# Inverse transform over n1 by even and odd rows, with stacked high and low parts, in a Fourier and maxout kernel

## The chip, the cores and the metric

The kernel runs on one core of one Trainium2 chip. The metric is the device time of one execution in microseconds. Six names come up: TensorE (PE, with its weight loads as PEld), VectorE (DVE), ScalarE (ACT), GpSimd (POOL), and SyncE (SP), which issues most of the transfers.

## What is computed

For each of 8 batches of 3072 rows and 256 columns: a real Fourier transform along the rows, a complex product with a 256 x 256 matrix plus bias, a soft threshold, the inverse transform, and then a layer that takes the maximum of three products and multiplies it by a fourth matrix.

```python
X = np.fft.rfft(x, axis=1)
Yr = Xr @ w_r - Xi @ w_i + b_r
Yi = Xr @ w_i + Xi @ w_r + b_i
Yr = np.sign(Yr) * np.maximum(np.abs(Yr) - lam, 0.0)      # Yi likewise
y = np.fft.irfft(Yr + 1j * Yi, n=3072, axis=1)            # (8, 3072, 256)
t = y.reshape(24576, 256)
h = np.maximum(np.maximum(t @ w1, t @ w2), t @ w3)        # 768 columns
out = h @ w_out                                           # (24576, 256)
```

## The kernel before

The transform length is split as 3072 = 96 x 32 (n1 and n2). Stage a transforms over n1 (a 96-row product), stage b over n2 for each of the 96 rows in pairs, stage w multiplies by the complex matrix, stage q goes back over n2 and writes z to DRAM, and `inverse` goes back over n1 with the tables `ga_sb`. The layer of three products (`up`) and the last product (`down`) follow on the result y.

The main loop runs over 8 batches, 8 chunks of a batch (`NCH`; a chunk is 4 of the 32 n2, 384 rows of y) and 6 blocks of 128 of the 768 columns (`NF`). One step of it, called a slot, has three groups of `up` (i = 0, 1, 2) and a `down`. The stages a to q of later batches are fitted between these groups by a list of events: `at(pos, fn, i)` books a call at a position counted in slots, and `run_until(pos)` issues what is due. Batch 0 goes through the stages in a prologue ahead of the loop.

Nearly all products are made of a high and a low 16-bit part of each operand in three matmuls (`mm3`: high x high, high x low, low x high). A split is one ScalarE instruction for the high part and one VectorE instruction for the low part; the latter is put off by `later` and issued at the next `flush`, which stands after each group. `in_turn` keeps such a pair behind the last eviction of `up`. PSUM has the tags `up` (3 buffers), `dn` (2) and `ff` (3, for all stages by `ff_tile`).

The steps around the change:
- `load_z(b, c)` brings a chunk of z, 96 rows by 4 x 256, in one transfer on SP's queue; it is called at f = 1 of the chunk before.
- `split_z` makes zh and zl, at f = 3, in two pieces where a batch begins.
- `inverse` runs at f = 4, one half of d before the second group and the other behind the third. For each n2 it does `mm3` with z as the stationary operand (96 x 128) and 96 columns of `ga_sb` as the moving one. ScalarE and VectorE then write yh and yl straight from PSUM.
- Stage a has three forms: native 32-bit for the first two batches (q < `NATIVE`), split 32-bit parts for batches 2 and 3, and 16-bit parts from `HALF_X` on. The last needs the batch's scale ahead of time, so x is loaded twice, and `largest_m` takes the maximum in an earlier batch.
- SP issues its transfers in order. Besides z it has the loads of x (`xq`, `xm`) and a, and the moves of `ab` and `vb` between partitions in groups of four.

Of the kernel before, what the change touches and what calls it, by code (L numbers as in the profile page):

```python
# [20 lines left out]
SB, SG = 10, 20  # L21
# [4 lines left out]
def dft_tables():  # L26
# [53 lines left out]
    def halves(v, scale):  # L80
        v = v * 2.0**scale
        hi = v.astype(np.float16)
        return np.ascontiguousarray(np.stack([hi, (v - hi).astype(np.float16)], 1))

    return (
        fa.astype(np.float32),
        halves(ga, SG),
        halves(np.stack([np.concatenate([v, v]) for v in blocks], 1), SB),
# [6 lines left out]
def fourier_maxout_kernel(  # L95
# [14 lines left out]
    NATIVE = 2 * NCH  # L110
    HALF_X = 4 * NCH
    EARLY = NCH + 5
# [107 lines left out]
    def first_homes():  # L220
        g = ga_sb.bitcast(F32).rearrange("p i n m -> p (i n m)")
# [263 lines left out]
    def largest_m(q):  # L485
        b, q4 = divmod(q, NCH)
        with in_turn():
            nc.vector.tensor_reduce(
                out=batch(b, "x")[0:N1, q4:q4 + 1], in_=st.pop(("m", q)), axis=AX.X,
                op=ALU.max, apply_absolute_value=True,  # L490
            )
        if q4 == NCH - 1:
            scale_x(b, NCH)
            st[b, "xx"] = xx = small("xx", bufs=3)
            nc.vector.tensor_scalar(
                out=xx, in0=st[b, "sx"][0], scalar1=X_SCALE, scalar2=None, op0=ALU.mult
            )

# [329 lines left out]
    for q in range(EARLY, NB * NCH):  # L828
        b, i = divmod(q, NCH)
        p = i if b == 1 else 9 + 5.2 * i if b == 2 else (b - 2) * SLOTS + 5.6 * i + 2  # L830
        at(p - (3 if b == 1 else 5 if b == 2 else 8), load_x, q)
        at(p, split_x, q)
        at(p + 1, stage_a, q)
        if q >= HALF_X:
            p = (b - 3) * SLOTS + 5.6 * i + 5
            at(p - 4, load_m, q)
            at(p, largest_m, q)
    for b in range(1, NB):
        for k in range(-2, NJP + 1):
            p = 8 + 2.2 * (k + 2) if b == 1 else (b - 1) * SLOTS + 2.8 * (k + 2)  # L840
            for d, fn, i in (
# [22 lines left out]
    def split_z(b, pieces=1):  # L864
        zh = fft.tile([96, NQ, D], F16, name="zh", bufs=1)
        zl = fft.tile([96, NQ, D], F16, name="zl", bufs=1)
        w = NQ * D // pieces
        for i in range(pieces):
            with in_turn():
                split_later(  # L870
                    *(t.rearrange("p n d -> p (n d)")[:, i * w:i * w + w] for t in (zh, zl)),
                    st["zq"][:, i * w:i * w + w], st[b, "su"][0][0:96],
                )
        st["z"] = zh, zl

    def inverse(b, c, y=None, part=(0, KD)):
        zh, zl = st["z"]
        yh, yl = y or [ffn.tile([P, KD, NT], F16, name=n, bufs=2) for n in ("yh", "yl")]
        for h in range(*part):
            py = ff_tile("pi")  # L880
            for n2 in range(NQ):
                mm3(
                    py[:, n2 * N1:(n2 + 1) * N1], *(t[:, n2, h * P:(h + 1) * P] for t in (zh, zl)),
                    *(ga_sb[:, i, c * NQ + n2, :] for i in range(2)),
                )
                st["pi"] = st["mm"]
            split_later(
                *(t[:, h].rearrange("p (m n) -> p m n", n=NQ) for t in (yh, yl)),
                py[:, 0:NT].rearrange("p (n m) -> p m n", n=NQ), Y_SCALE,
            )  # L890
        return yh, yl
# [166 lines left out]
    for b in range(NB):  # L1058
        for c in range(NCH):
            nxt = (b, c + 1) if c + 1 < NCH else (b + 1, 0) if b + 1 < NB else None  # L1060
            for f in range(NF):
                pos = b * SLOTS + c * NF + f
                up(y, f, 0)
                flush()
                if nxt and f == 3:
                    split_z(nxt[0], 1 if nxt[1] else 2)
                if nxt and f == 4:
                    y_next = inverse(*nxt, None, (0, 1))
                run_until(pos - 2 / 3)
# [19 lines left out]
                run_until(pos)  # L1089
                if nxt and f == 1:  # L1090
                    load_z(*nxt)
# [37 lines left out]
```

## Time and profile before

| | us |
|---|---|
| median of 3 runs | 2025.78 (2024.03 to 2027.57) |
| the profiled execution | 2023.95 |
| its span in the profile | 2022.2 |
| TensorE busy | 2005.8 |
| VectorE busy | 1428.8 |
| ScalarE busy | 1046.5 |
| inverse, high part of y on ScalarE, 128 times | 61.9 |
| inverse, low part of y on VectorE, 128 times | 70.5 |

The profile is one execution on the chip. A group's line has the source line, the engine, the operation, output and inputs with their shapes, the count, the busy time in us and the mean ns of one, and after a second bar the idle time of the engine in front of it with what ended it. Matmuls are pipelined, so their durations overlap; how long TensorE takes for a run of them is read from the starts in the timeline. A line of windows gives a stretch, its length, the busy time of each engine with its count, the granted clock of TensorE, the share of the transfer engines, and GB/s.

### The profile page before, as it was taken

The page shows a single profiled execution, that of the slowest core. Times are in us where ns is not written, and L with a number is a line of the kernel's source. Part 1 is how long each engine was busy: PE and PEld are TensorE (multiplying, and loading weights), DVE is VectorE, ACT ScalarE, POOL GpSimd, SP SyncE. Part 2 cuts the span into 40 slices and gives each one's busy share as a digit, 9 for nine tenths or more (in the row PEclk, how much of TensorE's full clock was granted, in tenths as well). Part 3 has the DMA queues.
Part 4 walks back from the last instruction along what each step waited for, and adds up shares of the span by engine and source line. Part 5 has one row for each costly group of instructions (what it writes and reads, how often), then busy time and mean ns, then how long its engine had stood idle before and what let it go on. Part 6 is the DMA issues. An engine that isn't in the chain of part 4 may idle for free.

```text
span 2022.2 us, 40241 instructions
## 1 busy us (share of the span) xinstructions
PE 2005.8 (99%) x15822; PEld 1406.3 (70%) x15822; DVE 1428.8 (71%) x2733; ACT 1046.5 (52%) x2052; POOL 20.5 (1%) x75
## 2 busy tenths in 40 slices
PE   9999999999999999999999999999999999999999
PEld 5757777777766777676776777767777677776666
DVE  3887886688866877677875788757776577754454
ACT  5755654455545555455544565545554454543333
POOL 0000000000000000000000000000000000000000
PEclk9999999999999999999999999999999999999999
DMA  9744443355433454345442454333442333311110
GB/s 302 206 134 134 126 121 93 112 137 137 110 113 96 120 142 110 93 108 135 127 113 87 122 138 117 103 107 82 128 113 61 89 94 93 82 53 32 32 32 24
DMA packets 203664, 220.34 MB, mean 109 GB/s; under 512 B 20659, under 2 KB 178995, under 8 KB 203379
## 3 DMA queue, kind: packets, MB, share of 16 engines
q1 hardware_dynamic: 142707, 142.24, 26.9%
q10 hardware_dynamic: 59744, 72.11, 11.2%
q0 software_dynamic: 1024, 3.41, 0.5%
q8 instruction: 125, 2.05, 0.4%
q14 instruction: 64, 0.52, 0.1%
HBM read 99.98 MB, written 75.50 MB: 87 GB/s over the span
## 4 chain that ended last, share of the span: by engine, by line
PE 96%; DVE 2%; DMA 1%; ACT 1%; issue 0%; SPq 0%; ACTq 0%; DVEq 0%
PE pu L174 18%; PE pu L172 18%; PE pu L173 18%; PE pd L174 6%; PE pd L173 6%; PE pd L172 6%; PE py L172 3%; PE py L174 3%; PE py L173 3%; PE px L674 2%; PE pa L531 1%; PE pi L174 1%; PE pi L172 1%; PE pi L173 1%; PE pa L172 1%; PE pa L173 1%
## 5 line engine op out<-in xcount | busy, mean ns | idle before, releaser
L172 PE MATMUL pu<-yh,wuh 128*128 128x384 f16 x2304 | 751.8, 326 | 2.5 <-DVE c L905 1.0
L174 PE MATMUL pu<-yh,wul 128*128 128x384 f16 x2304 | 751.5, 326 | 0.0
L173 PE MATMUL pu<-yl,wuh 128*128 128x384 f16 x2304 | 751.3, 326 | 0.1
L166 ACT ACTIVATE hh<-h 128x384 f16<-128x384 f32 x384 | 200.4, 522 | 495.3 <-DVE h L908 494.1
L905 DVE TENSOR_TENSOR c<-pu,c 128x384 f32<-128x384 f32 x384 | 212.6, 554 | 251.5 <-PE pu L174 150.4
L174 PEld LDWEIGHTS <-wul 128*128 128x128 f16 x2304 | 225.4, 98 | 150.0 <-issue 1.0
L172 PE MATMUL pd<-woh,hh 128*128 128x256 f16 x1152 | 313.8, 273 | 0.0
L173 PE MATMUL pd<-wol,hh 128*128 128x256 f16 x1152 | 313.8, 273 | 0.0
L174 PE MATMUL pd<-woh,hh 128*128 128x256 f16 x1152 | 313.5, 273 | 0.0
L173 PEld LDWEIGHTS <-wuh 128*128 128x128 f16 x2304 | 225.7, 98 | 125.4 <-issue 4.1
L172 PEld LDWEIGHTS <-wuh 128*128 128x128 f16 x2304 | 225.6, 98 | 125.3 <-issue 4.6
L167 DVE SCALAR_TENSOR_TENSOR hh<-h,hh 128x384 f16<-128x384 f32 x384 | 213.6, 556 | 138.9 <-ACT hh L166 136.6
L902 ACT ACTIVATE c<-pu 128x384 f32<-128x384 f32 x384 | 187.2, 488 | 187.6 <-PE pu L174 165.8
L908 DVE TENSOR_TENSOR h<-pu,c 128x384 f32<-128x384 f32 x384 | 211.8, 551 | 46.5 <-PE pu L174 42.6
L172 PE MATMUL py<-wch,tt 128*128 128x256 f16 x504 | 137.4, 273 | 0.0
L174 PE MATMUL py<-wch,tt 128*128 128x256 f16 x504 | 137.3, 272 | 0.0
L173 PE MATMUL py<-wcl,tt 128*128 128x256 f16 x504 | 137.3, 272 | 0.0
L172 PEld LDWEIGHTS <-hh 128*128 128x128 f16 x1152 | 112.7, 98 | 33.8 <-issue 0.3
L173 PEld LDWEIGHTS <-hh 128*128 128x128 f16 x1152 | 112.7, 98 | 33.4
L174 PEld LDWEIGHTS <-hh 128*128 128x128 f16 x1152 | 112.7, 98 | 13.7 <-DVE hh L167 0.5
L937 ACT ACTIVATE o<-pd,s1u 128x256 f32<-128x256 f32 x191 | 82.7, 467 | 75.1 <-PE pd L174 35.5
L167 DVE SCALAR_TENSOR_TENSOR zl<-zq,s0u,zh 96x1024 f16<-96x1024 f32 (+1 forms) x72 | 83.0, 1157 | 4.3 <-ACT zh L166 4.2
(219 smaller groups left out, 2635.6 us busy)
## 6 DMA issues: line engine op xcount, KB each, us to landing
z_d<-zs ACTq DMA_DIRECT2D x96, 256.0 KB, 2.9
out_dram<-o ACTq DMA_DIRECT2D x190, 128.0 KB, 2.1
zq<-z_d SPq DMA_DIRECT2D x63, 384.0 KB, 3.9
ab<-a_d SPq DMA_DIRECT2D x84, 256.0 KB, 4.1
ab<-ab SPq DMA_DIRECT2D x336, 64.0 KB, 2.1
xq<-in_x_dram SPq DMA_DIRECT2D x55, 384.0 KB, 3.9
a_d<-aq ACTq DMA_DIRECT2D x53, 384.0 KB, 3.3
vb<-vb SPq DMA_DIRECT2D x308, 64.0 KB, 2.4
```

The costliest lines, as they stand in the source:

```text
L166: nc.scalar.activation(out=hi, in_=src, func=AF.Copy, scale=scale)
L167: later(lambda: low(nc.vector.scalar_tensor_tensor(out=lo, in0=src, scalar=scale, in1=h, op0=ALU.mult, op1=ALU.subtract)))
L172: nc.tensor.matmul(o, lh, rh, start=start, stop=False, **kw)
L173: nc.tensor.matmul(o, lh, rl, start=False, stop=False, **kw)
L174: st["mm"] = nc.tensor.matmul(o, ll, rh, start=False, stop=stop, **kw)
L531: nc.tensor.matmul(pa[0:96], fr, xp, start=True, stop=True)
L674: nc.tensor.matmul(pv[:, h, :, g // 2, g % 2], ah[:, g // 2, g % 2, h * P:(h + 1) * P], mb_sb[:, i, 4 * kb + g].rearrange("p (c m) -> p c ...
L902: st["act"] = nc.scalar.activation(out=c1, in_=p, func=AF.Copy)
L905: st["dve"] = nc.vector.tensor_tensor(out=c1, in0=p, in1=c1, op=ALU.max)
L908: st["dve"] = nc.vector.tensor_tensor(out=h32, in0=p, in1=st["c1"], op=ALU.max)
L937: nc.scalar.activation(out=o, in_=pd[t], func=AF.Copy, scale=st[b, "su"][1])
```

## The change

The inverse table has a symmetry over n1: moving n1 by 48 multiplies the term of frequency k1 by +1 or -1 as k1 is even or odd. The changed `inverse` uses it. The 96 rows of z are sorted into 48 of even and 48 of odd frequency; each kind is multiplied by 48 columns of the table only, and the two results are added for the first 48 values of n1 and subtracted for the others.

High and low part of 48 rows fill 96 partitions together. So one matmul with `ga`'s high part takes both high x high and low x high, and a second one with its low part takes the rest (low x low comes along). For a half of d this is 2 kinds x 4 n2 x 2 = 16 matmuls of 48 columns where 4 x 3 = 12 of 96 columns stood. To stack the parts, `load_z` places the rows by kind in two transfers, `split_z` splits as before, and four transfers in SBUF bring the halves of zh and zl together. Behind the matmuls ScalarE copies the even result, VectorE forms sum and difference, ScalarE makes yh of them and VectorE yl.

In the loop `load_z` moves from f = 1 to f = 0, `split_z` from f = 3 to f = 2, the first half of the inverse from f = 4 to the end of f = 3, and the second from the end of f = 4 to behind its second group. The events are set a little closer (2.72 slots for 2.8 a step, 2.13 for 2.2 in batch 1). Batch 3's stage a changes to 16-bit parts (`HALF_X`), and the scale of such a batch is computed one slot behind the last maximum (`scale_m`).

```diff
+    m = np.arange(96)
+    ga = np.stack([ga[m % 4 >= 2, :, 0:48], ga[m % 4 < 2, :, 0:48]], 1)
...
-        halves(ga, SG),
+        np.concatenate([halves(ga, SG)] * 2),
...
-    HALF_X = 4 * NCH
+    HALF_X = 3 * NCH
...
-    ga_sb = const.tile([96, 2, N2, N1], F16, name="ga_sb")
+    ga_sb = const.tile([96, 2, 2, N2, N1 // 2], F16, name="ga_sb")
...
-        if q4 == NCH - 1:
-            scale_x(b, NCH)
...
+    def scale_m(b):
+        scale_x(b, NCH)
...
         if q >= HALF_X:
-            p = (b - 3) * SLOTS + 5.6 * i + 5
+            p = 9 + 5 * i if b == 3 else (b - 3) * SLOTS + 5.5 * i + 5
             at(p - 4, load_m, q)
             at(p, largest_m, q)
+            if i == NCH - 1:
+                at(p + 1, scale_m, b)
...
-            p = 8 + 2.2 * (k + 2) if b == 1 else (b - 1) * SLOTS + 2.8 * (k + 2)
+            p = 8 + 2.13 * (k + 2) if b == 1 else (b - 1) * SLOTS + 2.72 * (k + 2)
...
     def load_z(b, c):
...
-        for r in (slice(0, 88), slice(88, 96)) if b == c == 0 else (slice(0, 96),):
-            st["lz"] = ld = nc.sync.dma_start(out=zv[r], in_=batch(b, "z")[r, c * NQ:(c + 1) * NQ, :])
+        rows = batch(b, "z").rearrange("(j m) n d -> j m n d", m=4)
+        for j in (slice(0, 22), slice(22, 24)) if b == c == 0 else (slice(0, 24),):
+            for e in range(2):
+                st["lz"] = ld = nc.sync.dma_start(
+                    out=zv[48 * e + 2 * j.start:48 * e + 2 * j.stop],
+                    in_=rows[j, 2 - 2 * e:4 - 2 * e, c * NQ:(c + 1) * NQ, :],
+                )
...
     def split_z(b, pieces=1):
...
+        both = [
+            fft.tile([P, 2, D], F32, name="ze", tag=tag, bufs=3)[0:96].rearrange("p a d -> p (a d)").bitcast(F16)
+            for tag in ("vl", "vh")
+        ]
...
+            def move(cols=cols):
+                for i, t in enumerate((zh, zl)):
+                    for e in range(2):
+                        nc.sync.dma_start(
+                            out=both[e][48 * i:48 * i + 48, cols], in_=t[48 * e:48 * e + 48, cols]
+                        )
+
+            later(move)
...
     def inverse(b, c, y=None, part=(0, KD)):
...
-            for n2 in range(NQ):
-                mm3(
-                    py[:, n2 * N1:(n2 + 1) * N1], *(t[:, n2, h * P:(h + 1) * P] for t in (zh, zl)),
-                    *(ga_sb[:, i, c * NQ + n2, :] for i in range(2)),
+            for e in range(2):
+                for n2 in range(NQ):
+                    for i in range(2):
+                        st["pi"] = st["mm"] = nc.tensor.matmul(
+                            pv[:, e, n2], st["z"][e][:, n2, h * P:(h + 1) * P],
+                            ga_sb[:, i, e, c * NQ + n2], start=i == 0, stop=i == 1,
+                        )
...
+            nc.scalar.activation(
+                out=even, in_=py[:, 0:NT // 2], func=AF.Copy, scale=Y_SCALE
+            )
+
+            def halves(h=h, even=even, y32=y32, pv=pv):
...
+                for e in range(2):
+                    nc.vector.scalar_tensor_tensor(
+                        out=yv[:, e], in0=pv[:, 1], scalar=(1 - 2 * e) * Y_SCALE, in1=ev,
+                        op0=ALU.mult, op1=ALU.add,
+                    )
+                nc.scalar.activation(
+                    out=yh[:, h], in_=y32, func=AF.Copy
                 )
...
+                later(lambda: low(
+                    nc.vector.tensor_tensor(out=yl[:, h], in0=y32, in1=yh[:, h], op=ALU.subtract)
+                ))
+
+            later(halves)
...
-                if nxt and f == 3:
+                if nxt and f == 2:
                     split_z(nxt[0], 1 if nxt[1] else 2)
-                if nxt and f == 4:
-                    y_next = inverse(*nxt, None, (0, 1))
                 run_until(pos - 2 / 3)
                 up(y, f, 1)
                 flush()
+                if nxt and f == 4:
+                    inverse(*nxt, y_next, (1, KD))
...
-                if nxt and f == 4:
-                    inverse(*nxt, y_next, (1, KD))
+                if nxt and f == 3:
+                    y_next = inverse(*nxt, None, (0, 1))
...
-                if nxt and f == 1:
+                if nxt and f == 0:
                     load_z(*nxt)
```

More of the change, by code (lines that the diff above doesn't have):

```diff
@@ L220, in first_homes @@
     def first_homes():
-        g = ga_sb.bitcast(F32).rearrange("p i n m -> p (i n m)")
+        g = ga_sb.bitcast(F32).rearrange("p i e n m -> p (i e n m)")
         w = wuh.bitcast(F32).rearrange("p i k f -> p (i k f)")
@@ L491, in largest_m @@
             )
-        if q4 == NCH - 1:
-            scale_x(b, NCH)
[L494 to L497, printed above, removed]
+    def scale_m(b):
+        scale_x(b, NCH)
+        st[b, "xx"] = xx = small("xx", bufs=3)
+        nc.vector.tensor_scalar(
+            out=xx, in0=st[b, "sx"][0], scalar1=X_SCALE, scalar2=None, op0=ALU.mult
+        )
     def split_x(q):
@@ L864, in split_z @@
     def split_z(b, pieces=1):
-        zh = fft.tile([96, NQ, D], F16, name="zh", bufs=1)
-        zl = fft.tile([96, NQ, D], F16, name="zl", bufs=1)
+        zh = fft.tile([96, NQ * D], F16, name="zh", bufs=1)
+        zl = fft.tile([96, NQ * D], F16, name="zl", bufs=1)
+        both = [
+            fft.tile([P, 2, D], F32, name="ze", tag=tag, bufs=3)[0:96].rearrange("p a d -> p (a d)").bitcast(F16)
+            for tag in ("vl", "vh")
+        ]
         w = NQ * D // pieces
         for i in range(pieces):
+            cols = slice(i * w, i * w + w)
             with in_turn():
[L870 to L874, printed above, removed]
+                split_later(zh[:, cols], zl[:, cols], st["zq"][:, cols], st[b, "su"][0][0:96])
+            def move(cols=cols):
[5 more added lines that the diff above has]
+            later(move)
+        st["z"] = [t.rearrange("p (n d) -> p n d", n=NQ) for t in both]
     def inverse(b, c, y=None, part=(0, KD)):
-        zh, zl = st["z"]
         yh, yl = y or [ffn.tile([P, KD, NT], F16, name=n, bufs=2) for n in ("yh", "yl")]
@@ L880, in inverse @@
             py = ff_tile("pi")
-            for n2 in range(NQ):
-                mm3(
-                    py[:, n2 * N1:(n2 + 1) * N1], *(t[:, n2, h * P:(h + 1) * P] for t in (zh, zl)),
-                    *(ga_sb[:, i, c * NQ + n2, :] for i in range(2)),
-                )
[L886 to L890, printed above, removed]
+            pv = py[:, 0:NT].rearrange("p (e n m) -> p e n m", e=2, n=NQ)
+            for e in range(2):
[5 more added lines that the diff above has]
+                        )
+            even, y32 = (
+                fft.tile([P, 2, D], F32, name=name, tag=tag, bufs=bufs).rearrange("p a d -> p (a d)")[:, 0:n]
+                for name, tag, bufs, n in (("ye", "vh", 3, NT // 2), ("y32", "aj", 2, NT))
+            )
+            nc.scalar.activation(
+                out=even, in_=py[:, 0:NT // 2], func=AF.Copy, scale=Y_SCALE
+            )
+            def halves(h=h, even=even, y32=y32, pv=pv):
+                ev = even.rearrange("p (n m) -> p n m", n=NQ)
+                yv = y32.rearrange("p (e m n) -> p e n m", e=2, n=NQ)
+                for e in range(2):
+                    nc.vector.scalar_tensor_tensor(
+                        out=yv[:, e], in0=pv[:, 1], scalar=(1 - 2 * e) * Y_SCALE, in1=ev,
+                        op0=ALU.mult, op1=ALU.add,
+                    )
+                nc.scalar.activation(
+                    out=yh[:, h], in_=y32, func=AF.Copy
+                )
+                later(lambda: low(
+                    nc.vector.tensor_tensor(out=yl[:, h], in0=y32, in1=yh[:, h], op=ALU.subtract)
+                ))
+            later(halves)
         return yh, yl
```

## The prediction

> **What bounds the kernel now.** I read the page's busy times first, then its chain that ended last, then the table of windows, then the waits of TensorE.
>
> ```profile
> span 2022.2 us, 40241 instructions
> PE 2005.8 (99%) x15822; PEld 1406.3 (70%) x15822; DVE 1428.8 (71%) x2733; ACT 1046.5 (52%) x2052; POOL 20.5 (1%) x75
> ...
> PE 96%; DVE 2%; DMA 1%; ACT 1%; issue 0%; SPq 0%; ACTq 0%; DVEq 0%
> ```
>
> TensorE is busy in 99% of the span, and 96% of the chain that ended last is TensorE. So the time goes by what TensorE has to stream, plus a few stalls.
>
> ```profile
> 103.90:107.50 3.60, 1.52 (x25) 1.15 (x26) 1.43 (x3) 3.23 (x6) 0.00 (x0) 1.00 0.70 218
> 107.50:111.70 4.20, 4.09 (x14) 1.95 (x14) 3.06 (x5) 0.82 (x2) 0.00 (x0) 0.59 0.83 230
> ...
> 460.00:560.00 100.00, 100.00 (x826) 71.17 (x825) 83.38 (x146) 55.42 (x110) 1.84 (x8) 1.00 0.44 119
> ...
> 1860.00:1960.00 100.00, 100.00 (x764) 69.10 (x763) 50.69 (x87) 37.02 (x73) 0.00 (x0) 1.00 0.11 33
> ```
>
> The columns are the stretch, its length, and the busy time of PE, PEld, DVE, ACT and POOL, then the granted clock. In the middle and at the end TensorE is full while VectorE is at 83 and 51 us of 100. The exception is the passage from the prologue into the main loop (103.9 to 107.5 us): TensorE works 1.52 of 3.60 us there, and then runs with a mean clock of 0.59 for 4.2 us. That passage is the first inverse, and it lies bare on the path.
>
> **Term 1: the inverse's matmuls.** One half (128 columns of d) of one chunk takes 12 matmuls of 96 columns now, and 16 of 48 columns after. There are 64 chunks of two halves, so 128 halves.
>
> ```profile
> 1001.03 0.21 PE L172 MATMUL pi<-ga_sb,zh 96*128 96x96 f16 x1
> ...
> 1001.50 0.21 PE L174 MATMUL pi<-ga_sb,zl 96*128 96x96 f16 x1
> ...
> 1006.10 0.63 PE L674 MATMUL px<-mb_all,ab 128*128 128x64 f16 x16
> 1006.57 0.33 PE L172 MATMUL pu<-yh,wuh 128*128 128x384 f16 x1
> ...
> L172 PE MATMUL pi<-ga_sb,zh x512: 204/206/216, 105.1 to 1988.1; 96*128 96x96 f16 x171
> ```
>
> The first column is the start. Durations overlap, so I take start to start: 11 steps in 0.47 us are 42.7 ns for 96 columns; 16 matmuls of 64 columns take 0.47 us, 29.4 ns each. The 512-column ones (rows under term 2) take 1.29 us for six, 215 ns. These three lie on one line: 0.414 ns a column plus 2.9 ns, since 29.4 + 448 x 0.414 = 215, and the line gives 42.7 at 96. At 48 columns it would give 22.8 ns, but no row is under 64 columns. Each matmul brings its own weight load; the third-last group's durations, 204 to 216 ns, show that a load which cannot hide (the matmul after a wait) costs about 10 ns, so it hides under 22 as well. The bounds are the line, 22.8 ns, and the shortest spacing that the trace has, 29.4 ns. I take 25: nearer to the line, which holds at three sizes, but not on it, as a start-to-start floor could sit just under 64 columns unseen. Per half: 12 x 42.7 = 0.512 us now, 16 x 25 = 0.400 after. Saving 0.112 us x 128 = **14.4 us** (18.9 by the line, 5.4 by the row of 64).
>
> The Trainium skill ("TensorE: Matmul & The Clock Gate", Back-to-back issue gap) speaks against the line: it says that starts never come closer than about 25 ns however few columns there are. By it a half is 0.400 us and the saving 14.4 us; no row of this trace is short enough to show it.
>
> **Term 2: stage a of batch 3.** Sixteen pairs of three products move from 32-bit to 16-bit parts.
>
> ```profile
> 584.71 0.53 PE L172 MATMUL pa<-xhl,fh 96*96 96x512 f32 x1
> ...
> 586.23 0.35 PE L257 MATMUL pt<-id_sb,col 96*128 96x96 f32 x2
> ...
> 623.50 0.38 PE L172 MATMUL pa<-xhl,zeros 96*96 96x512 f16 x1
> ...
> 624.79 0.33 PE L172 MATMUL pu<-yh,wuh 128*128 128x384 f16 x1
> ```
>
> Six products take 1.52 us in 32 bits and 1.29 in 16 bits: 0.23 us for each of 8 quads, **1.8 us**. In return eight more loads of x (384 KB) and eight reductions of 1.2 us come into batch 0, and sixteen of 0.67 us leave batch 1: VectorE does 1.2 us less in all, but some 10 us of it 50 slots earlier.
>
> **Term 3: the scale of a batch** is taken a slot after the last maximum instead of right behind it.
>
> ```profile
> PE pt L257 <- DVE col L255: 2.5, 4, 1.1
> ...
> PE pz L172 <- DMA vb<-vb: 0.2, 1, 0.2
> ```
>
> TensorE waits 2.5 us in four places for that column (cause, total, times, longest). With the reduction done long before, only VectorE's queue remains in front of it: I take **1.0 us** of gain, between 0 and 2.5.
>
> **What VectorE and ScalarE get.**
>
> ```profile
> L167 DVE SCALAR_TENSOR_TENSOR yl<-pi,yh 128x384 f16<-128x384 f32 x128 | 70.5, 551 | 13.9 <-ACT yh L166 13.7
> L690 DVE SCALAR_TENSOR_TENSOR s<-px,s 128x256 f32<-128x256 f32 x77 | 31.8, 414 | 0.0
> L687 ACT ACTIVATE s<-px 128x256 f32<-128x256 f32 x77 | 29.0, 377 | 0.0
> L166 ACT ACTIVATE yh<-pi 128x384 f16<-128x384 f32 x128 | 61.9, 484 | 15.9 <-PE pi L174 15.1
> L166 ACT ACTIVATE hh<-h 128x384 f16<-128x384 f32 x384 | 200.4, 522 | 495.3 <-DVE h L908 494.1
> ```
>
> A sum or difference of 192 columns, from the rows of 384 and 256: 414 - 64 x (551 - 414)/128 = 345 ns (estimate). Two of them and a subtraction of 384 (551) are 1.24 us a half against 0.55 now: +0.69 us, 88 us over 128 halves; VectorE goes from 71% to about 75%, and from 83 to about 88 in its fullest stretch. ScalarE gets an even copy of 192 (377 - 64 x (484 - 377)/128 = 323 ns) and reads its yh from SBUF (522 for 484): +0.36 us a half, 46 us. I cost both at nothing, since TensorE covers them with 100 of 100 us; without that cover they would cost up to 88 us. In the chain behind a half, the even copy, sum, difference, yh and yl come to 0.32 + 0.69 + 0.52 + 0.55 = 2.1 us of work, where 1.04 stand now; the second half starts two thirds of a slot (3.3 us of a mean slot of some 5 us) earlier, which covers it. The new wait stands on ScalarE, where yh waits for VectorE's difference; behind it are the copies of pu that TensorE's next groups need, and three buffers of pu, about a slot, lie between.
>
> **Term 4: the moves on SP's queue.** Stacking high and low parts needs four transfers SBUF to SBUF a chunk (eight where a batch begins, as there are two pieces), and the load of z becomes two.
>
> ```profile
> 193.75 2.54 SPq L793 DMA_DIRECT2D vb<-vb  x4
> ...
> zq<-z_d SPq DMA_DIRECT2D x63, 384.0 KB, 3.9
> ...
> vb<-vb SPq DMA_DIRECT2D x308, 64.0 KB, 2.4
> ```
>
> Four such moves hold SP for 2.54 us, about 0.65 apart, and land 2.4 us after issue. Per chunk of some 31 us that is 5 x 0.65 = 3.2 us more on SP, which has room. But the moves wait in SP's order for the low parts of z, and behind them stand the loads of x and a, and the moves of ab and vb. The nearest case is vb: four moves behind a ScalarE and a VectorE step, read 1.6 slots after the step; it cost TensorE 0.2 us in 84 times (row above). Between split_z (after the first product of f = 2) and the first half (end of f = 3) lie 1.67 slots, 8.3 us; needed are 1.14 + 1.27 us for zh and zl, 2.5 of issue and 2.4 of landing, 7.3 us. So it holds in a chunk, with 1 us to spare. Where a batch begins, eight moves need 5.2 us of issue alone: 0.7 + 5.2 + 2.4 = 8.3 us, nothing to spare, seven times. I take **+2 us** for this and the first chunk, whose VectorE is nearly full (bounds 0 and 10).
>
> **Term 5: the first inverse**, which nothing covers.
>
> ```profile
> 104.37 0.71 ACT L166 ACTIVATE zh<-zq,s0u 96x512 f16<-96x512 f32 x1
> ...
> 105.11 1.41 DVE L167 SCALAR_TENSOR_TENSOR zl<-zq,s0u,zh 96x512 f16<-96x512 f32 x2 [2.69 <-ACT zh L166]
> ...
> 107.50 0.48 PE L172 MATMUL pu<-yh,wuh 128*128 128x384 f16 x2 [0.41 <-ACT yh L166]
> ```
>
> Now the first zh starts at 104.37 and the main loop at 107.50. After, zh's first move can go at 105.1; the eighth is issued 7 x 0.65 later, at 109.65, and lands at 112.05. Then the last matmuls (0.3), even copy 0.32, sum and difference 0.69, yh 0.52: the main loop starts at about 113.9, 6.4 us later. The second half comes 0.6 later than now; the load's doubled last piece and a longer half-speed stretch of the clock can add, the kernel's own weight preparation on VectorE in these microseconds can take some back. I take **+7 us** (3 to 11).
>
> **Sum**: -14.4 - 1.8 - 1.0 + 2 + 7 = -8.2 us. The profiled execution took 2023.95 us (span 2022.2), which gives 2015.75; it lies 1.8 us under the median of the runs, 2025.78, which gives 2017.6. I put the median's: **2017.6 us**.
>
> **Rivals.** The measurement tells 0.2% (4 us) from no change, so faster means under 2021.7.
> 1. The line holds to 48 columns: -18.9 in place of -14.4, 2013.1 us. For it: three sizes on it, and a weight load of about 10 ns. Against it: nothing under 64 columns is in the trace.
> 2. The 29.4 ns are a floor, so that 48 columns cost as much as 64: -5.4 in place of -14.4, 2026.6 us, no change. For it: the saving then comes from four matmuls more at a shorter time. Against it: 29.4 lies on the line, which a floor need not.
> 3. Slower: the moves come late, since SP's queue holds them behind others. One group of four vb moves ahead of them is 2.54 us, which makes them 1.5 us late after the spare 1 us; if that meets every third chunk it is 0.5 us a chunk, 31 us over 63 chunks, and the time is 2049. The change is slower from 0.2 us a chunk on ((8.2 + 4)/63). Against it: the 0.2 us in all for vb, which is placed alike.
> 4. The change does less than it says: VectorE at 88 of 100 delays the evictions of pu in batches 0 to 2, some 0.2 us a chunk over 20 chunks, +4 us: 2021.6.
>
> **How the numbers follow.** Forecast 0.36, the line (1) 0.28, the floor at 29.4 (2) 0.14, late moves (3) 0.14, evictions (4) 0.08. Forecast and line are faster, the floor is the same, 4 is split between faster and same, 3 is slower; the forecast's own edge (first inverse at +11) gives some to the same side. Faster 0.65, same 0.19, slower 0.16. The range takes the line with the cheapest startup, 2025.78 - 18.9 - 1.8 - 2.5 + 3 = 2005.6, and the floor with the dearest, 2025.78 - 5.4 - 1.8 + 0 + 2 + 11 = 2031.6; outside remains most of rival 3. Range **2006 to 2031**.
>
> **What would show each step.** Start to start of the new matmuls: 25 ns a pair, a half in 0.40 us. Six products of batch 3 in 1.29 us. The first product of the main loop at about 114 us in place of 107.5. VectorE near 1517 us and ScalarE near 1092. TensorE's waits: few on DMA of the stacked z and on yh; late moves would stand there. I am wrong if the spacing is 29 or more, if TensorE waits over 10 us for the stacked z, or if the main loop starts after 119.

## The result, and the profile after

| | before | after |
|---|---|---|
| median of the runs, us | 2025.67 (4 runs, 2024.03 to 2027.57) | 2053.55 (4 runs, 2053.14 to 2055.21) |
| profiled execution, us | 2023.95 | 2055.21 |
| its span, us | 2022.2 | 2053.4 |
| TensorE's first product of the main loop, us from the start | 107.5 | 120.7 |

The ratio is 1.0137 (95% interval 1.0125 to 1.015): the kernel became 28 us slower, where 8 us less were forecast. The time lies 22 us above the range.

The head of the page of the changed kernel: span, busy times, and shares of the chain that ended last.

```profile
span 2053.4 us, 42317 instructions
PE 2002.3 (98%) x16334; PEld 1391.9 (68%) x16334; DVE 1508.0 (73%) x2982; ACT 1080.3 (53%) x2180; POOL 23.5 (1%) x75
...
PE 77%; DVE 7%; DMA 5%; ACT 5%; issue 3%; ACTq 2%; SPq 1%; DVEq 0%
```

TensorE's share of the chain fell from 96% to 77%. Its busy time hardly moved: a matmul's row overlaps the next by about 0.16 us (0.33 us long, next start 0.16 us later), so that busy time hides short gaps; the chain shows what it hides. VectorE's and ScalarE's totals are near the forecast (1517 and 1092). The table of windows of the changed kernel, same columns as before:

```profile
106.50:120.66 14.16, 2.04 (x34) 1.43 (x33) 2.85 (x7) 4.09 (x8) 0.00 (x0) 0.64 0.64 192
117.86:124.10 6.24, 4.56 (x35) 2.60 (x36) 4.33 (x8) 1.96 (x5) 0.00 (x0) 0.50 0.79 253
...
1860.00:1960.00 100.00, 98.76 (x786) 67.10 (x784) 54.71 (x101) 40.08 (x83) 0.00 (x0) 1.00 0.17 50
```

The passage into the main loop takes 14 us with 2 us of TensorE work in it, and TensorE's clock stands at half beyond its end. In the last batch, where VectorE works 55 us of 100, TensorE is no longer full: 98.76 us. TensorE's waits (cause, total, times, longest):

```profile
PE pi L905 <- DMA ze<-zl: 23.5, 25, 7.2
PE px L677 <- DMA ab<-ab: 4.4, 3, 1.6
```

The stacked z (`ze`) is the first cause, and the moves of `ab`, which do not stand among the waits of before, the second.

**Where 31.2 us went** (span against span). The main loop starts 13.2 us later; the rest takes 1932.7 us where it took 1914.7, 18.0 more. To split the latter, take for each matmul of the loop the time to the next one's start, subtract the usual value (the lower quartile) of its output and shape, and add up what exceeds it by more than 6 ns. These stalls come to 13.8 us before and 45.4 after, of which 18.0 stand in front of the inverse's matmuls, nearly all for `ze` (59 places), and 6.8 in front of `px` (12), 5.1 of these for `ab`. The usual spacings add up to 13.3 us less after. So the saving came; against it stand about 31 us of new stalls in the loop, and the late start.

Of the 18.0 us, 10.7 fall to the seven chunks in which the next batch's z is stacked, 3.7 to the seven other chunks of the last batch, and 3.6 to ten more chunks. By what ended them, the stalls sort into 22.8 us for transfers (1.1 before) and 13.9 for VectorE (5.4 before, and 2.8 in the kernel of experiment 2 that has all of the change but the inverse). Most of the others are short gaps that the profile puts down to no wait.

**One late chunk of the last batch**, where nothing else runs. The timeline of the changed kernel (start, duration), first ScalarE:

```profile
1884.89 0.48 ACT L944 ACTIVATE c<-pu 128x384 f32<-128x384 f32 x1
...
1885.69 1.15 ACT L168 ACTIVATE zh<-zq,s0u 96x1024 f16<-96x1024 f32 x1 [0.32 <-ACT c L944]
```

The same stretch on SP:

```profile
1886.87 1.28 SPq L890 DMA_DIRECT2D ze<-zh  x2
1888.24 1.17 SPq L890 DMA_DIRECT2D ze<-zl  x2
```

And on TensorE:

```profile
1883.45 0.33 PE L174 MATMUL pu<-yh,wuh 128*128 128x384 f16 x1
...
1890.08 0.27 PE L175 MATMUL pd<-wol,hh 128*128 128x256 f16 x1
1890.19 0.27 PE L176 MATMUL pd<-woh,hh 128*128 128x256 f16 x1
1890.73 0.36 PE L905 MATMUL pi<-ga_sb,ze 96*128 96x48 f16 x8 [0.27 <-DMA ze<-zl]
1890.93 0.32 PE L174 MATMUL pu<-yh,wuh 128*128 128x384 f16 x1
```

The first product of f = 2 ends about 1883.45, where the second begins, and there `split_z` is issued. The inverse could start 0.11 us (the step between the two `pd` rows) after 1890.19, at 1890.30: 6.85 us. But zh stands behind an eviction of `up` and starts 2.24 us late, at 1885.69; from there splits, issues and landing take until 1890.73, 5.04 us. Together 7.28 us are needed, and TensorE loses 0.43. A slot here lasts 4.08 us (a chunk of 24.47 us before, by six), so 1.67 slots are 6.8 us. The last seven chunks take 24.59 to 25.34 us in place of the 24.25 that they take without the moves (below).

No transfer ahead of them held these moves: over all chunks the first one is issued 0.03 us behind the end of zh by the median, and 0.4 us at most. They are late by their own chain. In batches 0 to 6 the cover is 9.3 us by the median, and most chunks there have z in time; while the first chunk of batches 1 to 7 runs it is 6.8 us, as in the whole last batch.

**Where a batch begins**, z is split in two pieces with four moves each. ScalarE, SP and TensorE in the changed kernel, shortly ahead of batch 6 (lines of three views):

```profile
1596.79 1.33 ACT L168 ACTIVATE zh<-zq,s0u 96x512 f16<-96x512 f32 x2 [0.30 <-ACT c L944]
...
1597.54 1.89 SPq L890 DMA_DIRECT2D ze<-zh  x2
...
1602.06 1.17 SPq L890 DMA_DIRECT2D ze<-zl  x2
```

```profile
1602.02 0.32 PE L176 MATMUL pu<-yh,wul 128*128 128x384 f16 x1
1604.14 0.38 PE L905 MATMUL pi<-ga_sb,ze 96*128 96x48 f16 x8 [1.79 <-DMA ze<-zl]
```

`split_z` is issued at 1594.55. zh again starts 2.24 us behind it, after the eviction; the eight issues go from 1597.54 to 1603.23, and the matmuls of the second piece start at 1604.14, 9.6 us behind `split_z`. They could have started 0.16 us after 1602.02, so TensorE loses about 2 us. Over the seven places the second piece is there 8.9 to 9.6 us behind `split_z`.

**A chunk in the middle**, SP's part of the timeline of the changed kernel:

```profile
417.83 1.23 SPq L890 DMA_DIRECT2D ze<-zh  x2
419.24 1.14 SPq L890 DMA_DIRECT2D ze<-zl  x2
420.47 3.35 SPq L588 DMA_DIRECT2D ab<-ab  x4
```

TensorE's part, a little later:

```profile
425.60 0.28 PE L677 MATMUL px<-mb_all,ab 128*128 128x64 f16 x4
427.21 0.51 PE L677 MATMUL px<-mb_all,ab 128*128 128x64 f16 x12 [1.33 <-DMA ab<-ab]
```

Here z is in time, but its four issues take 2.6 us of SP, and the four moves of `ab` right behind them land 1.33 us too late for `px`. SP has room on average; what it did not have was room just there.

**The start.** SP's timeline of the changed kernel around the first inverse:

```profile
99.69 6.62 SPq L866 DMA_DIRECT2D zq<-z_d  x4
...
110.72 1.27 SPq L890 DMA_DIRECT2D ze<-zh  x2
112.08 1.18 SPq L890 DMA_DIRECT2D ze<-zl  x2
113.36 0.65 SPq L987 DMA_DIRECT2D mb_all<-in_dft_b_dram  x1
114.07 1.23 SPq L890 DMA_DIRECT2D ze<-zh  x2
115.40 1.17 SPq L890 DMA_DIRECT2D ze<-zl  x2
```

ScalarE's:

```profile
109.97 0.72 ACT L168 ACTIVATE zh<-zq,s0u 96x512 f16<-96x512 f32 x1 [2.40 <-DMA zq<-z_d]
```

TensorE's:

```profile
114.14 0.48 PE L905 MATMUL pi<-ga_sb,ze 96*128 96x48 f16 x8 [7.20 <-DMA ze<-zl]
117.86 1.12 PE L905 MATMUL pi<-ga_sb,ze 96*128 96x48 f16 x24 [3.24 <-DMA ze<-zl]
120.66 0.80 PE L174 MATMUL pu<-yh,wuh 128*128 128x384 f16 x2 [1.68 <-ACT yh L925]
```

zh starts at 109.97 in place of 104.37, 5.6 us later; from zh to the main loop it is 10.7 us in place of 3.13, 7.6 more. Of the 5.6 us, 3.1 come from the prologue ahead of it (the last store of z is issued at 100.52 us in place of 97.41); its mean clock around 32 us shows one part of that, here in the windows of the changed kernel:

```profile
31.50:35.50 4.00, 3.68 (x13) 3.35 (x14) 1.00 (x3) 1.18 (x3) 0.00 (x0) 0.57 0.93 319
```

The granted clock is 1.00 in this stretch before, but 0.57 as here in the profile of the rest alone too (experiment 2), which has nothing of the new inverse. I don't put these 3.1 us to the change; that the spans differ by 31.2 us and the medians by 27.9 fits that. Over the profiles of this document the last store of z is issued anywhere from 96.3 to 103.0 us, so the start is better read from that store to the main loop: 10.1 us before, 20.1 after, 19.2 to 22.3 in the six other kernels that keep the moves there, and 14.6 without them (experiment 1).

### The profile page after: what moved, and what is told of

It is laid out like the page before. It is cut to its first block, busy times and chain, and to the rows that moved or that the text cites. A ratio compares the mean times of both kernels' runs of the same rounds, so it can differ in the third digit from the quotient of the medians.

```text
span 2053.4 us, 42317 instructions
## 1 busy us (share of the span) xinstructions
PE 2002.3 (98%) x16334; PEld 1391.9 (68%) x16334; DVE 1508.0 (73%) x2982; ACT 1080.3 (53%) x2180; POOL 23.5 (1%) x75
## 3 DMA queue, kind: packets, MB, share of 16 engines
q0 software_dynamic: 1024, 3.41, 0.5%
## 4 chain that ended last, share of the span: by engine, by line
PE 77%; DVE 7%; DMA 5%; ACT 5%; issue 3%; ACTq 2%; SPq 1%; DVEq 0%
PE pu L176 15%; PE pu L175 15%; PE pu L174 15%; PE pd L176 5%; PE pd L174 5%; PE pd L175 5%; DMA ze<-zl 3%; PE pi L905 2%; PE py L174 2%; PE py L176 2%; PE py L175 2%; PE px L677 2%; DVE zl L169 2%; ACTq L980 2%; ACT o L979 1%
## 5 line engine op out<-in xcount | busy, mean ns | idle before, releaser
L921 DVE SCALAR_TENSOR_TENSOR y<-pi,ye 128x192 f32<-128x192 f32 x256 | 112.0, 508 | 26.2 <-ACT ye L913 25.6
```

Source lines behind the costliest of these rows:

```text
L921: nc.vector.scalar_tensor_tensor(out=yv[:, e], in0=pv[:, 1], scalar=(1 - 2 * e) * Y_SCALE, in1=ev, op0=ALU.mult, op1=ALU.add,)
```

## The experiments

The theory after the result: the moves (four a chunk, eight where a batch begins) are the whole loss, by their latency, by SP's order and by the bare start. Its rivals: VectorE, with the sums and differences; and the other parts of the change, the events set closer and batch 3 in 16 bits. All ratios are to the kernel before, with the 95% interval. "Stalls" are those of the main loop, worked out as above.

### 1. No moves

```diff
-            def move(cols=cols):
...
-            later(move)
-        st["z"] = [t.rearrange("p (n d) -> p n d", n=NQ) for t in both]
+        st["z"] = [t.rearrange("p (n d) -> p n d", n=NQ) for t in (zh, zl)]
```

> The changed kernel without the four transfers that stack the parts: the even kind is multiplied with the high part alone and the odd kind with the low part, so part of the computation is left out; all matmuls, sums and schedule stay. Changed kernel 2053.6 us, before 2025.7. If the moves cost the time (they come late at the chunks, hold up the ab moves behind them on SP, and stand bare at the start): the inverse's waits (18 us in the main loop) and those of px (7 us) go, and the main loop starts about 7 us earlier; 2021 us, range 2015 to 2028. If VectorE's longer work or the closer events cost it: at most the start is saved, 2045 us.

Measured: 2023.15 us, 0.9987 (0.9977 to 0.9996), stalls 21.3 us, main loop from 111.7 us. TensorE's waits in this kernel begin so:

```profile
PE pi L893 <- ACT zh L168: 4.8, 2, 4.5
PE pa L175 <- DVE xhl L169: 3.5, 4, 1.1
PE pt L259 <- DVE col L257: 3.1, 5, 0.9
```

With every other instruction of the change in place (the two buffers `ze` go with the moves), 30.4 us are gone, the wait for `ab` with them, and the last chunks take 24.25 us: 0.22 less than before. Against the kernel before, the moves are the loss. VectorE has the same work here (1505 us busy), so it does not make these 30 us. But its work is not free: the stalls are still 21.3 us, where the rest of the change alone has 12.1 (experiment 2), and 13.6 of them end with VectorE, where that kernel has 2.8. With the start 4 us longer (14.6 us from the last store of z, 10.7 in that kernel) this uses up the saving: the time is no lower than the 2022.94 us of the rest alone.

### 2. The parts of the change apart

e2_inverse_alone keeps the new inverse and takes batch 3's 16-bit parts and the late scale back:

```diff
-    HALF_X = 3 * NCH
+    HALF_X = 4 * NCH
...
+        if q4 == NCH - 1:
+            scale_m(b)
...
-            p = 9 + 5 * i if b == 3 else (b - 3) * SLOTS + 5.5 * i + 5
+            p = (b - 3) * SLOTS + 5.6 * i + 5
...
-            if i == NCH - 1:
-                at(p + 1, scale_m, b)
```

> The changed kernel with batch 3's stage a in 32-bit parts again, and the scale and the maxima as before; the new inverse stays. If the moves cost the time: the 1.8 us of batch 3 are lost and the rest stays, 2055 us (2051 to 2058). If the maxima in batch 0 and the loads of x for them crowd VectorE and SP: 2042 us or less.

e3_rest_alone is the reverse of it: the kernel before with `HALF_X`, `scale_m` and the closer events of the changed one.

> The kernel before with everything of the change but the inverse: batch 3's stage a in 16-bit parts, the scale a slot later, events at 2.72 and 2.13 slots. If the moves cost the time: 1.8 us of batch 3 and about 1 us of the scale's waits are gained, 2023 us (2020 to 2026). If the closer events and the earlier maxima cost it: 2036 us or more.

Measured: the inverse alone 2055.71 us, 1.0146 (1.013 to 1.0162); the rest alone 2022.94 us, 0.9985 (0.9975 to 0.9995), stalls 12.1 us. Both are as expected for the moves. The loss goes with the inverse. The rest gains 2.9 us against the runs of before beside it (2025.79), and the stalls in front of `pt`, which waits for the column of the scale, fall from 3.7 to 0.4 us in it.

### 3. The first half of the inverse later

If the moves are only just late, a third of a slot more should free most of it. The first half goes from the end of f = 3 to behind the first product of f = 4:

```diff
+                if nxt and f == 4:
+                    y_next = inverse(*nxt, None, (0, 1))
                 run_until(pos - 2 / 3)
...
-                if nxt and f == 3:
-                    y_next = inverse(*nxt, None, (0, 1))
```

> The changed kernel with the first half of the inverse a third of a slot later, behind the first group of f = 4 in place of the end of f = 3. If the moves land just too late at ordinary chunks (waits of 0.3 to 0.6 us for ze in the trace, two at batch starts of 1 to 2 us): these waits go in ordinary chunks, 8 to 12 us less, 2044 us; the start's 13 us stay. If the moves' place on SP's queue is the cost, through ab and x: no change, 2053 us.

Measured: 2041.94 us, 1.0076 (1.0057 to 1.0095); the stalls in front of the inverse fall from 18.0 to 8.3 us, all of these where a batch begins, and the last chunks take 24.25. TensorE's waits in it:

```profile
PE pi L905 <- DMA ze<-zl: 15.4, 13, 7.0
PE px L677 <- DMA ab<-ab: 3.6, 4, 1.4
```

Over 10 us of what is left for `ze` lie ahead of the main loop. `ab` waits as before: moving the reader does not move SP's queue. Experiments 4 to 7 build on this kernel.

### 4. Sums in another order of columns

The sums took 508 ns each where 345 were estimated. They write every fourth element, since the output is ordered by n1 and the PSUM by n2. Here they write straight on, and the reads behind them take the step instead:

```diff
-                yv = y32.rearrange("p (e m n) -> p e n m", e=2, n=NQ)
+                yv = y32.rearrange("p (e n m) -> p e n m", e=2, n=NQ)
...
-                    out=yh[:, h], in_=y32, func=AF.Copy
+                nc.scalar.activation(out=yhv, in_=yn, func=AF.Copy)
...
-                    nc.vector.tensor_tensor(out=yl[:, h], in0=y32, in1=yh[:, h], op=ALU.subtract)
+                    nc.vector.tensor_tensor(out=ylv, in0=yn, in1=yhv, op=ALU.subtract)
```

> The kernel with the first half a third of a slot later (2041.9 us, VectorE's sums 508 ns each), with sum and difference written in the order of the matmuls' columns, and the reordering left to ScalarE's and VectorE's reads behind them. If the strided output makes the sums slow, they take about 345 ns, VectorE is busy some 40 us less, and if VectorE is not what limits, the time stays: 2041 us (2037 to 2044). If VectorE's length delays TensorE: 2035 us or less.

Measured: 2045.57 us, 1.01 (1.0083 to 1.0117), no gain and 1.6 us above the expected range. The groups of the changed kernel:

```profile
L921 DVE SCALAR_TENSOR_TENSOR y<-pi,ye 128x192 f32<-128x192 f32 x256 | 112.0, 508 | 26.2 <-ACT ye L913 25.6
L929 DVE TENSOR_TENSOR yl<-y,yh 128x384 f16<-128x384 f32 x128 | 70.9, 554 | 22.3 <-ACT yh L925 22.1
...
L925 ACT ACTIVATE yh<-y 128x384 f16<-128x384 f32 x128 | 66.7, 521 | 81.9 <-DVE y L921 81.6
```

Those of this one:

```profile
L929 ACT ACTIVATE yh<-y 128x384 f16<-128x384 f32 x128 | 108.8, 863 | 84.9 <-DVE y L921 84.9
L931 DVE TENSOR_TENSOR yl<-y,yh 128x384 f16<-128x384 f32 x128 | 103.6, 812 | 36.0 <-ACT yh L929 35.8
L921 DVE SCALAR_TENSOR_TENSOR y<-pi,ye 128x192 f32<-128x192 f32 x256 | 79.1, 350 | 29.9 <-ACT ye L913 29.7
```

350 ns confirms the estimate for columns in order. But VectorE wins 33 us on the sums and loses 33 on the low parts, and ScalarE loses 42: the stepped access is paid where it is put. The expected 40 us less on VectorE missed, so this run could not show what a lighter VectorE is worth.

### 5. Four moves where eight stood

Where a batch begins, z comes in two pieces with four moves each. Here one set of four stands behind both:

```diff
-            def move(cols=cols):
...
-            later(move)
+        def move():
+            for i, t in enumerate((zh, zl)):
+                for e in range(2):
+                    nc.sync.dma_start(out=both[e][48 * i:48 * i + 48], in_=t[48 * e:48 * e + 48])
+
+        later(move)
```

> The kernel with the first half a third of a slot later (2041.9 us), with four moves a chunk always, behind both pieces, where eight stood at the start and at the seven batch starts. If eight issues of 0.65 us on SP set the landing there: the inverse's waits at batch starts (8 us in the profile of the kernel with the half later) shrink by 5 and the main loop starts 2 us earlier, 2035 us (2031 to 2038). If the waits come from the load of z and not from the moves: 2041 us.

Measured: 2035.55 us, 1.0043 (1.0028 to 1.0058), 6.4 us less than experiment 3. The stalls in the loop in front of the inverse are down to 1.1 us and those of `px` from 7.2 to 3.8, for `ab` from 4.4 to 1.2: the moves' share of the loss in the loop was mostly the eight of them at the batch starts and a third of a slot. The other half of the expectation missed: the start did not get shorter. From the last store of z to the main loop it takes 20.1 us here and 19.2 in experiment 3: from zh on it is 10.1 us in place of 10.8, but zh itself came 1.7 us later, which no run explains. All stalls of the loop still come to 25.0 us; of what is left of the loss, the largest part should lie at the start.

### 6. Other queues for the moves

If SP's order is the trouble, another queue should end the wait for `ab`. e7_pool_queue gives the moves to GpSimd's queue (`nc.gpsimd.dma_start` for `nc.sync.dma_start`).

> The kernel with the first half a third of a slot later (2041.9 us), with the stacking moves on GpSimd's queue. If the moves delay the transfers behind them on SP: the waits of px for ab (7.2 us in that profile) fall under 1.5 us, 2034 us (2029 to 2038), unless GpSimd issues more slowly than SP. If px waits for another reason (closer events, VectorE): they stay, 2041 us.

e8_act_queue has one set of four, the high part's moves on ScalarE's queue and the low part's on SP:

```diff
...
+        def move(i, q):
+            t = (zh, zl)[i]
+            for e in range(2):
+                q.dma_start(out=both[e][48 * i:48 * i + 48], in_=t[48 * e:48 * e + 48])
+
+        move(0, nc.scalar)
+        later(lambda: move(1, nc.sync))
```

> The kernel with one set of four moves a chunk, of which the two of the high part go on ScalarE's queue right behind the split that makes them, and the two of the low part on SP. If the number of issues on SP ahead of the last move and ahead of ab sets the waits: the last move is issued 1.3 us earlier everywhere; px's waits fall to 3 us, the inverse's to 3 us, 2030 us (2025 to 2035). If ScalarE's own evictions suffer from issuing: TensorE's waits for c and yh grow, 2040 us or more.

Measured on GpSimd's queue: 2084.66 us, 1.0291 (1.0271 to 1.0311). TensorE's waits in that kernel:

```profile
PE pi L905 <- DMA ze<-zl: 47.5, 31, 9.6
```

The stalls of `px` do fall, from 7.2 to 1.6 us, and none is left for `ab`, so SP's order was the cause of these. But those in front of the inverse rise from 8.3 to 42.9 us in 154 places. A late chunk of this kernel, GpSimd and TensorE (two views):

```profile
1914.23 1.00 POOL L890 DMA_DIRECT2D ze<-zl  x2 [0.23 <-DVE zl L169]
```

```profile
1918.33 0.36 PE L905 MATMUL pi<-ga_sb,ze 96*128 96x48 f16 x8 [1.31 <-DMA ze<-zl]
```

GpSimd's busy time goes from 24 to 172 us with the issues, but they are not slow, and hardly late: one takes 0.50 us, where SP takes 0.58, and the first comes 0.29 us behind zh by the median. What is late is the landing. The last issue here starts at 1914.73, and TensorE has to wait until 1918.33, 3.6 us; in the late chunk of the changed kernel above, on SP's queue, it was 1.9 us. Over all waits for `ze` that time has a median of 3.9 us here, with 7.2 at most, and of 1.9 in the changed kernel. Why a move lands later from GpSimd's queue, no run shows.

On ScalarE's and SP's queue: 2042.18 us, 1.0078 (1.0063 to 1.0093), not the 2030 expected. `px` stalls for 0.1 us only, but TensorE's waits show the next one:

```profile
PE pi L905 <- DMA ze<-zl: 15.0, 5, 12.1
PE pz L174 <- DMA vb<-vb: 5.7, 4, 1.9
```

The stalls of `pz` come to 9.3 us in all, 6.4 of them for `vb`, and those of the inverse to 4.3. The other reading, ScalarE's own evictions, does not show: the stalls of `pu` for its `c` are 0.8 us, near the 1.0 of experiment 5. SP's order was a cause for `ab`, but neither of the two other queues that were tried was better than four moves on SP.

### 7. The first chunk as before

The kernel of experiment 5, with the first chunk alone done by the old inverse and a small table of its own for it:

```diff
-    load_z(0, 0)
-    split_z(0, 2)
-    y = inverse(0, 0)
+    y = first_inverse(g0_sb)
```

> The kernel with four moves a chunk always (2035.6 us), with the first chunk's inverse alone done as before: one load in the old order, no moves, 96 columns, a small table of its own. If the bare start costs what the traces show (from the last store of z to the main loop 10.1 us before, about 20 us since): 10 us less, 2025.5 us (2022 to 2029). If VectorE's preparation of weights in these microseconds sets the end of the first chunk anyway: 2032 us or more.

Measured: 2022.6 us, 0.9979 (0.997 to 0.9989), 13.0 us less than experiment 5, give or take 4 by the two intervals; the main loop starts at 108.2 us. From the last store of z to the main loop it takes 10.3 us in place of 20.1, so some 10 us of the 13 are seen at the start itself. With it, the batch starts and the third of a slot mended, the change is faster than before, but not than its rest alone (2022.94 us, experiment 2). Stalls in the loop stay at 23.5 us, 9.7 above before and 11.4 above the rest alone: `pu` 4.8, `pt` 3.8, `pa` in 16 bits 3.6, `px` 3.1, `pz` 2.5. By what ended them, 13.0 us are VectorE's and 4.9 transfers'.

### 8. 32 columns

Is 25 ns the floor between two starts, or is it something of 48 columns? In the kernel without moves, the second product of each pair streams 32 of its 48 columns.

> The kernel without moves (2023.2 us), where the second product of each pair, the one with the table's low part, streams 32 columns of 48, so part of the computation is left out. If 25 ns is a floor start to start: still 25 ns a matmul and 2023 us. If the line of 0.414 ns a column holds below 64: 16 ns for the short ones, 1024 x 9 ns = 9 us less, 2014 us.

Measured: 2020.49 us, 0.9973 (0.9962 to 0.9983). Its TensorE timeline; each of the first two rows has four of 48 and four of 32 columns in turn:

```profile
1911.40 0.36 PE L893 MATMUL pi<-ga_sb,zh 96*128 96x48 f16 x8
1911.61 0.35 PE L893 MATMUL pi<-ga_sb,zl 96*128 96x48 f16 x8
1911.81 0.32 PE L174 MATMUL pu<-yh,wuh 128*128 128x384 f16 x1
```

Eight starts take 0.20 to 0.21 us, as the eight of 48 columns alone did at 1890.73 to 1890.93. Start to start it is 25 ns after one of 48 as after one of 32. (The rows are grouped by the first shape, so 32 columns don't show in them.) A line through 64 and more columns would give 16 ns at 32. The floor stands at 25 ns. The median is 2.7 us below that of experiment 1, where a floor gives no difference and the line 9 us; the two intervals overlap. The Trainium skill ("TensorE: Matmul & The Clock Gate", Back-to-back issue gap) gives about 25 ns as the least, and this trace agrees.

### 9. Each kind loaded twice, no moves

The moves can be had in the load: each kind of z is loaded to two groups of partitions, and the split writes high parts in the one and low parts in the other. First chunk as in experiment 7; the schedule is that of the changed kernel, and z has one buffer of its own.

> The changed kernel's schedule without any move: each kind of z is loaded twice, to partitions 0 to 47 and 64 to 111, the high part is made on all of them at once and the low part in place on the upper ones; the table has 16 rows of zeros between; the first chunk as before. ScalarE and VectorE each split twice as much (1.1 and 1.3 us more a chunk). If the moves and the start are the whole cost: the stalls of the kernel without moves (21 us in the loop) and the start of before, 2018 us (2014 to 2023), faster than both kernels. If VectorE's 80 us more or the doubled loads on SP bring their own waits: 2030 us or more.

Measured: 2031.21 us, 1.0032 (1.0021 to 1.0044); the main loop starts at 107.7 us, but the stalls are 34.4 us, 12.3 of them `pa` for VectorE's low part. Busy times of this kernel:

```profile
PE 1997.7 (98%) x16326; PEld 1389.8 (68%) x16326; DVE 1577.2 (78%) x3034; ACT 1133.5 (56%) x2234; POOL 27.0 (1%) x76
```

VectorE has some 70 us more and ScalarE 53 (against the changed kernel), and this is not hidden. The stalls that end with VectorE come to 23.9 us, where experiment 1, with VectorE at 1505 us, has 13.6 and the rest alone, at 1422, has 2.8: in these three kernels TensorE waits the longer for VectorE, the more work that has, though it is busy for 70 to 78% of the span only.

### 10. Stage a later

Of experiment 7's stalls those of `pa` and `pt` wait for VectorE. Here stage a of batches 2 to 7 comes half a slot later:

```diff
-        at(p + 1, stage_a, q)
+        at(p + (1.5 if b > 1 else 1), stage_a, q)
```

> The kernel with four moves a chunk and the first chunk as before (2022.6 us), with stage a of batches 2 to 7 half a slot later behind its split. If TensorE's waits for the split x (3.6 + 1.7 us in that profile) come from VectorE's longer queue, as the splits end just too late: they fall under 1.5 us, 2018.5 us (2015 to 2021). If a later stage a only moves the wait to the loads of a behind it: 2022 us or more.

Measured: 2021.8 us, 0.9977 (0.9968 to 0.9986). Stalls of `pa` for the 16-bit parts fall from 3.6 to 1.2 us and those of `pt` from 3.8 to 0.5, but those of `px` rise from 3.1 to 6.5; the sum goes from 23.5 to 23.0. The time expected, 2018.5 us, was not reached: the wait moved on, though not to the loads of a but to ScalarE. The first of this kernel's waits is the one that took their place:

```profile
PE px L679 <- ACT aq L539: 3.2, 5, 0.7
```

It has the lowest median of the kernels that do the whole computation, but its interval overlaps that of the rest alone (experiment 2), so whether the inverse in its best form adds a gain to the rest is open.

## Why the prediction was wrong, step by step

**What bounds the kernel** was read rightly. What follows from it was not drawn: a full TensorE has no slack of its own, so any new wait in front of it is paid in full.

**The balance.** Forecast were 8.2 us less, measured 27.9 more, 36 us apart. By the profiles the moves cost some 24 us of stalls in the loop (45.4 without 21.3, experiment 1) where 2 were booked for them; the inverse's work beside the moves costs 9 (21.3 against 12.1) where nothing was booked; the start costs 10 where 7 were booked; and 3.1 are the prologue's own.

**Term 1, 25 ns a matmul: right.** Spacing and floor are as taken; a chunk of the last batch without waits falls from 24.47 to 24.25 us, 0.22 x 64 = 14.1 us against 14.4. The second rival, a floor at 29 ns, and the first, the line, are out.

**Terms 2 and 3, -2.8 us together: right** where they stand alone (-2.9, experiment 2). In the changed kernel the wait for the scale's column is back (`pt` stalls 3.4 us), since VectorE's queue is longer there.

**VectorE and ScalarE at no cost: totals right, cost wrong.** VectorE was at 1508 us for 1517 forecast, 86 us above the rest alone (1422.4) where 88 were booked. A sum took 508 ns for 345, since its output steps through memory, but sum and difference stand next to each other and overlap, as VectorE's timeline of the changed kernel has them:

```profile
1892.18 0.86 DVE L921 SCALAR_TENSOR_TENSOR y<-pi,ye 128x192 f32<-128x192 f32 x2 [0.96 <-ACT ye L913]
```

That is 0.86 us for both where 0.69 were booked. The step that failed here is "I cost both at nothing, since TensorE covers them with 100 of 100 us". A share of busy time does not show what stands in front of what in VectorE's queue: the stalls that end with VectorE are 13.9 us in the changed kernel, 13.6 in experiment 1, 13.0 in experiment 7, and 2.8 in the rest alone. The fourth rival had VectorE's cost, at 4 us, but at the evictions of `pu` (5.5 us of stalls in experiment 1 as in the rest alone); it came at the splits of x (`pa`) and the column of the scale (`pt`). No run with a lighter VectorE shows how much of it could be won back.

**Term 4, +2 us for the moves: the step that failed most.** The term was mis-sized, at 2 us for some 24, in three places.
- Where a batch begins, "0.7 + 5.2 + 2.4 = 8.3 us, nothing to spare, seven times" left out that zh waits 2.2 us behind an eviction before the first move can go. The second piece takes 8.9 to 9.6 us; 10.7 us of stalls stand there, and four of the eight moves taken away gave 6.4 us.
- In "1.67 slots, 8.3 us; needed are ... 7.3 us", the need was right as a sum (7.28 us in the chunk above), though of other pieces: the moves of zh start behind zh and not behind zl, and the 2.2 us come in here too. The cover was taken from a mean slot of 5 us. But a slot of the last batch is 4.08 us, as 24.47 us a chunk in the trace of before would have told, and there the cover is 6.8 us and not 8.3. That cost 3.7 us in the last batch and 3.6 in other chunks.
- I had `ab` named as standing behind the moves without asking what reads it next: `px` stalls for 6.8 us, 5.1 of them for `ab`.

The third rival came out near the measured time, 2049 us with a chance of 0.14, but by another mechanism: there the moves were late since SP's queue held them behind others. They were not held (0.03 us by the median), so the nearness is luck; SP's order cost time the other way round, to what stands behind the moves. What spoke against late moves, "0.2 us in all for vb", came from four moves with nothing new in front of them in SP's order.

**Term 5, +7 us for the first inverse: right in kind, somewhat too small.** From the last store of z to the main loop it is 10.0 us more, inside the bounds of 3 to 11, where 6.4 were worked out. (The 13.2 us by which the main loop starts later hold 3.1 of the prologue.) zh came 2.5 us later, and 3.2 in the kernel without moves, so this is not theirs: the load became two transfers a piece. (With the load of before, in experiment 7, it is 0.2.) The issues took 0.7 us more than seven times 0.65, since between the two sets of moves SP had a load of `mb_all` to issue; the landing was 0.5 shorter, and the work behind it 1.0 longer. TensorE, idle for 7.2 and 3.24 us, had half its clock until 124.1 us, into the main loop.

**The signs named** were fit to tell: spacing under 29 ns (so the forecast's gain was real), over 10 us of wait for the stacked z, and a main loop after 119 us. The last two came in. The third is the weakest: with the same first inverse the main loop starts at 115.5 us in the profile of experiment 3, mostly since the prologue ends earlier there.

## What to carry to other kernels

A change that saves time on a full engine by adding a transfer is priced by the transfer's whole chain (wait for the engine in front, issue, landing) against the shortest stretch of the schedule that has to cover it, not against a mean one; here that was the last batch, with nothing else in it, and the first chunk of the others. On a queue served in order, ask for each new issue what stands behind it and who reads that next. What happens once and bare, ahead of the loop, can keep its old form: here that alone was worth about 10 us by the profiles and 13 by the medians. And an engine that is busy three quarters of the time can still make the full one wait: price what stands behind the new work in its queue, not its total.

## What the runs showed of the hardware

- TensorE starts a matmul at most every 25 ns, with 48 as with 32 columns and with a new weight load each time (experiment 8).
- A stepped access costs VectorE about as much on either side: 508 for 350 ns where it writes 192 columns in steps of 16 bytes, twice a half, and 812 for 554 where it reads 384 of them out of order. ScalarE's copy of 384 columns takes 863 for 521 ns where it reads them out of order (experiment 4).
- A longer bare start costs more clock. The granted clock stood at half for 13.65 us (110.45 to 124.1 us) after the change, for 3.41 us (108.25 to 111.66) before it. In the profiles of experiments 2 to 6 that keep all the moves at the start it is 13.65 us five times and 17.07 once (on GpSimd's queue); without moves it is 6.83 and 10.24 us; with the first inverse of before it is nothing, 3.41 or 6.83 us. Within rounding, all of these are multiples of 3.41 us.
- A move from GpSimd's queue is issued in 0.50 us and one from SP's in 0.58, but where TensorE waited for the last one, it came 3.9 us after the issue by the median from GpSimd's and 1.9 us from SP's; the kernel became 43 us slower (experiment 6).
